# Third pair's loads behind the second pair's codes, and weight pieces 4 and 5 behind the first pair's, in a fused routing-attention and MLP kernel

## The chip, the cores and the metric

One core of a Trainium2 chip runs the whole kernel. The metric is device time in microseconds (us). The engines are called PE (TensorE, with PEld for its weight loads), DVE (VectorE), ACT (ScalarE), POOL (GpSimd) and SP (SyncE, which only issues DMAs here). Each runs its own instructions in the order in which the program lists them, and waits at an instruction until that one's inputs are there. So the program's order on each engine is part of the design, and this change moves that order about.

## The reference

Batch 4, 8 heads, 768 positions, head size 64, 16 clusters; d_model 512, d_ff 2048. Queries and keys are each assigned to the cluster whose centroid they resemble most, and a query attends only to keys of its own cluster. A two-layer block follows.

```python
q_assign = argmax(einsum('bhsd,hcd->bhsc', q_n, c_n))
k_assign = argmax(einsum('bhsd,hcd->bhsc', k_n, c_n))
mask = q_assign[:, :, :, None] == k_assign[:, :, None, :]
scores = where(mask, scale * (q @ k.T), -1e9)
attn = softmax(scores)
x = (attn @ v)            # heads side by side: (3072, 512)
h = x @ w_in
out = (h - tanh(h)) @ w_out
```

The weights come as 64-bit numbers, so a piece of them has to be turned into 32-bit numbers on the chip ("rounding").

## The kernel before

The work is tiled by pairs of heads: pair n is batch n // 4, heads 2p and 2p + 1. A pair's attention runs in six steps, written (n, half, s): half of the queries, and s = 0, 1, 2 for two 128-key blocks each. The list `steps` begins with the first halves of pairs 0 to 3 (steps 0 to 11), and one Python loop over it (L1031) writes out, for each step, the instructions of all engines in a fixed order. There is no scheduler: what the loop emits first on an engine runs first there.

A pair has to pass these stages before its steps:

- `load(n)` (L302): four DMAs on SP, 192 KB each, for q and k of both heads. In SBUF each head's rows are interleaved with the other's.
- `turn(n)` (L319): 12 PE transposes into two PSUM tiles `pt`, and two copies to SBUF (ACT for all but one).
- `similar(n)` (L337): PE products with the centroids, and an ACT copy.
- `route(n)` (L350): 3 PE transposes and four DVE operations, which leave each position's cluster code.
- `publish(n)` (L383): a PE transpose `pq`, a DVE cast, and a DMA on SP of the codes to DRAM (`q_codes`, 6 KB at most).
- `spread(0, 0)` (L398): for the first pair only, one DMA on SP brings the query codes back to all partitions as `row`. `select` (L467) then masks the exponentials on DVE.
- `spread_both(n)` (L406), for pairs 1 to 3: two DMAs on SP bring query and key codes back as `hot`; `one_hot(n)` (L414, DVE operations L418 and L422) turns them into factors, which PE adds to the scores (L454). A pair's scores cannot be finished before its `one_hot`.

A step of the loop emits, in this order: the scores of the next step (`begin`, L435, with ACT's exponentials L465), the ACT part of the day's weight pieces (`rest_of`), the products with v (`value`, `av`, L497), stage 0 (`turn`) if one is due, the sums of the weights (`sum_up`, `den`), then the rest: selects, the other stages, and the DVE part of the weight pieces (`round_piece`), each of which also fetches a piece three ahead through POOL's DMA queue (`fetch`, L209). `similar` (stage 1) comes ahead of the next step's scores.

When a stage is due stands in `ready` (L927 to L935): for pair n it is step `first_step + places[i]`, where i counts turn, similar, route, publish, spread_both, one_hot. Before the change the places of pair 2 are steps 0, 1, 1, 2, 2, 4, those of pair 3 steps 3, 4, 4, 5, 5, 7. The second pair's own stages are written out ahead of the loop, with `one_hot(1)` in step 1. For pair 3 `turn` also issues `load(4)` (L914). How many weight pieces are rounded in a step stands in `paces` (L1028).

The wait `gate` (L986) is a device that the kernel has already: a copy on POOL of one element of a loaded tile, so that the DMAs listed on POOL after it start only when that tile has landed. It holds the first three weight pieces behind the first pair's q and k.

Of the kernel before, what the change touches and what calls it, by code (L numbers as in the profile page):

```python
# [58 lines left out]
def kernel(  # L59
# [10 lines left out]
    nc = tc.nc  # L70
# [107 lines left out]
    def fast():  # L178
# [40 lines left out]
        def rest_of(at: int):  # L219
            if words == 2 and at < len(PIECES):  # L220
                rests[at] = restp.tile([P, FQ * P], U32, name="rest", tag="rest")
                added_words(PIECES[at][0], raws[at], rests[at])

        def round_piece(at: int):
            if words == 2:
                halved(PIECES[at][0], raws.pop(at), rests.pop(at))
            fetch(at + AHEAD)
# [74 lines left out]
        def load(n: int, what=(0, 1)):  # L302
            if n >= len(pairs):
                return
            b, p = pairs[n]
            for i in what:
                if i < 2:
                    pool, tag = (gp, "g") if b == 0 else (loads, f"x{i}")
                    t = raw_qk[n, i] = pool.tile([P, NCH, 2, D], F32, name=f"x{i}", tag=tag)
                else:  # L310
                    pool = vp0 if n in (2, 3) else vp
                    t = vals[n] = pool.tile([P, 2, NCH, D], F32, name="vals")
                for h in range(2):
                    nc.sync.dma_start(
                        t[:, :, h] if i < 2 else t[:, h],
                        (q, k, v)[i][b, 2 * p + h].rearrange("(p j) d -> p j d", p=P),
                    )
# [19 lines left out]
        def similar(n: int):  # L337

            ps = ps_f.tile([P, TB], F32, name="sim", tag="f")
            for i in range(2):  # L340
                for half in range(2):
                    r = (2 * i + half) * 2 * C
                    nc.tensor.matmul(  # L343
                        ps[r : r + 2 * C], lhsT=bd[:, pairs[n][1]],
                        rhs=turned[n, i][:, half], start=True, stop=True, tile_position=(0, r),
                    )
            sims[n] = rtp.tile([P, TB], F32, name="simt")
            nc.scalar.copy(out=sims[n], in_=ps)
# [25 lines left out]
        def summed(n: int, half: int):  # L374

            return n < HP and half == 0

        def masked(n: int, half: int):


            return summed(n, half) and n > 0

        def publish(n: int):  # L383

            sides = 2 if masked(n, 0) else 1
            G = HCH * 4 * sides
            ps = ps_f.tile([G, P], F32, name="pq", tag="f")
            nc.tensor.transpose(
                out=ps, in_=codes[n][:, 0:sides].rearrange("p i a h j -> p (i a h j)"), identity=ident
            )  # L390
            t = rtp.tile([G, P], BF16, name=f"qc{sides}")
            nc.vector.tensor_copy(out=t, in_=ps)
            q_codes[n] = dram.tile([sides, 2, 2, HCH * P], BF16, name=f"q_codes{sides}")
            nc.sync.dma_start(q_codes[n].rearrange("i a h (j p) -> (i a h j) p", p=P), t)

        rows, hots = {}, {}
# [9 lines left out]
        def spread_both(n: int):  # L406

            t = hots[n] = gp.tile([P, 2, 2, TB], BF16, name="hot", tag="g")
            for h in range(2):
                nc.sync.dma_start(  # L410
                    t[h * D : h * D + D], q_codes[n][:, :, h].unsqueeze(0).to_broadcast([D, 2, 2, TB])
                )
# [16 lines left out]
        def weight_tiles(n: int, half: int, s: int):  # L429
            if (n, half, s) == (0, 0, NS - 1):  # L430
                return [gp.tile([P, 2, TB], F32, name="e", tag="g") for _ in range(2)]
            t = ep.tile([P, 2, 2, TB], F32, name="e")
            return [t[:, i] for i in range(2)]

        def begin(step):  # L435
            n, half, s = step
            sc = {}
            for i in range(2):
                j = 2 * s + i
                sc[i] = ps_s.tile([P, 2, 512], F32, name="sc", tag="s")  # L440
                for h in range(2):
                    r = slice(h * D, h * D + D)
                    nc.tensor.matmul(  # L443
                        sc[i][:, h, 0:TB],
                        lhsT=turned[n, 1][r].rearrange("p a n -> p (a n)")[:, j * P : (j + 1) * P],
                        rhs=turned[n, 0][r, half], start=True, stop=not masked(n, half),
                    )
            for i in range(2):
                j = 2 * s + i
                out = sc[i][:, :, 0:TB]  # L450
                if masked(n, half):
                    for h in range(2):
                        r = slice(h * D, h * D + D)
                        nc.tensor.matmul(  # L454
                            sc[i][:, h, 0:TB],
                            lhsT=hots[n][r, 1].rearrange("p a n -> p (a n)")[:, j * P : (j + 1) * P],
                            rhs=hots[n][r, 0, half], start=False, stop=True,
                        )
                if summed(n, half):
                    if i == 0:  # L460
                        weights[n, half, s] = weight_tiles(n, half, s)
                    out = weights[n, half, s][i]
                else:
                    scores[n, half, j] = sc[i]
                nc.scalar.activation(out=out, in_=sc[i][:, :, 0:TB], func=ACT.Exp, scale=SCALE)  # L465
# [442 lines left out]
        def before(n: int):  # L908


            def turns():
                turn(n, 0, nc.scalar)
                turn(n, 1, nc.scalar)
                if n >= HP - 1:  # L914
                    load(n + 1)

            yield turns
            yield lambda: similar(n)
            yield lambda: route(n)
            yield lambda: publish(n)  # L920
            if masked(n, 0):
                yield lambda: spread_both(n)
                yield lambda: one_hot(n)
# [3 lines left out]
        ready = {}  # L927
        for n in range(2, len(pairs)):
            if n < HP:
                first_step, places = 3 * (n - 2), (0, 1, 1, 2, 2, 4)  # L930
            else:
                first_step = steps.index((n - 1, 0, 0) if n > HP else (n - 2, 1, 0))
                places = (-1, 0, 1, 3)
            for i, stage in enumerate(before(n)):
                ready.setdefault(first_step + places[i], {})[i] = stage  # L935
# [50 lines left out]
        gate = const.tile([P, 1], F32, name="gate")  # L986
# [13 lines left out]
        spread(0, 0)  # L1000
        rest_of(0)
        similar(1)
        load(2)
        rest_of(1)
        begin(steps[0])
        for _ in range(2):
            round_piece(rounding.pop(0))
        route(1)
# [1 line left out]
        begin(steps[2])  # L1010
        publish(1)
        spread_both(1)
        load(1, (2,))
        load(3)
        for n in range(2, HP):
# [9 lines left out]

        paces = dict(enumerate((0, 0, 1, 2, 0, 0, 2, 2, 1, 1, 1, 0, 3, 2, 2, 2, 2, 2, 2, 3, 2)))  # L1028
        late, divides, makers, later = [], [], [], {}
        fill, whole, spent, since, over = [], 0.0, 0.0, 0, 1  # L1030
        for at, (n, half, s) in enumerate(steps):  # L1031
# [108 lines left out]
        for t, bound in (  # L1140
# [7 lines left out]
            out=fits, in0=inverse, scalar1=MOST_INVERSE * words, scalar2=None, op0=ALU.is_le  # L1148
        )
        nc.vector.scalar_tensor_tensor(  # L1150
            out=fits, in0=inverse, scalar=words / SUM_MOST, in1=fits, op0=ALU.is_ge, op1=ALU.mult
        )
        checks = [fits, largest]
        if words == 2:
            nc.vector.tensor_scalar(
                out=smallest, in0=smallest, scalar1=HIGH_LEAST, scalar2=None, op0=ALU.is_ge
# [161 lines left out]
    with ExitStack() as cx, tc.manual_schedule():  # L1318
        fast()
# [35 lines left out]
```

## Time and profile before

| | us |
|---|---|
| three runs | 990.96, 991.83, 992.31 |
| median | 991.83 |
| span of the profiled execution | 990.3 |
| PE busy | 976.6 |
| PE weight loads | 467.0 |
| DVE busy | 531.4 |
| POOL busy | 499.7 |
| ACT busy | 321.7 |

A group's row in the profile gives start and length in us, engine, line, operation, output and inputs, how many instructions were merged, and in brackets how long the engine sat idle before and what ended that. SPq rows are DMA issues: their length is the time in which the queue took the descriptors, not that of the transfer. For these transfers the trace holds the moments at which each of a DMA's 16 shares reported completion; the last of them is its landing.

The 40 slices of the page are 24.8 us each. The change touches the first two or three.

### The profile page before, as it was taken

How to read it: one execution, taken by the hardware profiler on the slowest of the kernel's cores; microseconds unless marked ns; L12 is line 12 of the kernel's file. 1: busy time of each engine (PE TensorE's matmuls, PEld its weight loads, DVE VectorE, ACT ScalarE, POOL GpSimd, SP SyncE). 2: the span in 40 equal slices, each digit the busy share in tenths (PEclk: the TensorE clock that was granted, in tenths of full speed). 3: DMA queues.
4: the chain of work that ended last, by engine and by line, in shares of the span. 5: the costliest groups of instructions: out<-in, count | busy, mean ns of one | idle time of the engine just before them, and what ended most of it. 6: DMA issues, size and time to landing. Idle time of an engine off the chain costs nothing.

```text
span 990.3 us, 16579 instructions
## 1 busy us (share of the span) xinstructions
PE 976.6 (99%) x6444; PEld 467.0 (47%) x6444; DVE 531.4 (54%) x1017; ACT 321.7 (32%) x493; POOL 499.7 (50%) x346
## 2 busy tenths in 40 slices
PE   7999999999999999999999999999999999999997
PEld 4344443344443334444455555444455555444664
DVE  5547567448655667656554357655645336533011
ACT  5566564233442333343331222324341221122000
POOL 1015334444445464786777345676688345466600
PEclk9999999999999999999999999999999999999999
DMA  8854363125475724463536637344453232233321
GB/s 209 211 136 140 112 181 105 30 51 153 120 217 144 218 91 126 147 173 118 176 111 201 193 117 215 109 148 123 149 166 95 99 110 74 103 112 127 103 102 35
DMA packets 115977, 132.47 MB, mean 134 GB/s; under 512 B 62980, under 2 KB 95668, under 8 KB 113204
## 3 DMA queue, kind: packets, MB, share of 16 engines
q1 hardware_dynamic: 109508, 109.81, 37.3%
q0 software_dynamic: 6240, 21.50, 6.6%
q8 instruction: 53, 0.87, 0.4%
q14 instruction: 32, 0.26, 0.1%
q10 hardware_dynamic: 144, 0.03, 0.0%
HBM read 110.14 MB, written 21.17 MB: 133 GB/s over the span
## 4 chain that ended last, share of the span: by engine, by line
PE 96%; DVE 2%; DMA 1%; ACT 1%; issue 0%; POOL 0%; ACTq 0%; DVEq 0%
PE pd L855 22%; PE pu L804 21%; PE sc L443 14%; PE av L497 14%; PE o L628 8%; PE h L612 8%; PE pt L324 2%; PE den L537 2%; PE sim L343 1%; PE warm L294 1%; PE den L511 1%; DMA row<-q_codes 1%; PE pr L356 1%; DVE e L475 1%; PE den L518 0%
## 5 line engine op out<-in xcount | busy, mean ns | idle before, releaser
L488 POOL TENSOR_TENSOR sum<-sum,e 128x768 f32<-128x768 f32 x112 | 206.1, 1840 | 107.6 <-DVE e L475 103.8
L475 DVE SCALAR_TENSOR_TENSOR e<-row,code,sc 128x384 f32<-128x384 bf16 x336 | 185.2, 607 | 99.1 <-ACT sc L465 77.8
L855 PE MATMUL pd<-stream,G 128*64 128x256 f32 x1728 | 191.8, 379 | 0.0
L465 ACT ACTIVATE sc<-sc 128x768 f32<-128x768 f32 x168 | 125.9, 792 | 202.7 <-PE sc L443 187.9
L855 PEld LDWEIGHTS pd<-stream,G 128*64 128x64 f32 x1728 | 123.8, 137 | 67.4 <-issue 7.9
L443 PE MATMUL sc<-t,t 64*128 64x384 f32 x768 | 150.0, 509 | 0.9 <-ACT e L465 0.9
L497 PE MATMUL av<-e,vals 128*64 128x384 f32 x768 | 145.6, 498 | 1.8 <-DVE e L475 1.8
L799 POOL TENSOR_TENSOR G<-G,th 128x768 f32<-128x768 f32 (+1 forms) x51 | 88.0, 1738 | 98.6 <-ACT th L797 98.6
L804 PE MATMUL pu<-xT,stream 128*64 128x384 f32 x768 | 134.9, 488 | 0.7 <-DVE top L364 0.7
L804 PE MATMUL pu<-diff,stream 128*64 128x384 f32 x576 | 103.1, 487 | 0.0
L443 PEld LDWEIGHTS sc<-t,t 64*128 64x128 f32 x768 | 66.0, 186 | 74.8 <-issue 41.9
L484 POOL TENSOR_TENSOR sum<-e 128x768 f32<-128x768 f32 x28 | 56.8, 2028 | 74.6 <-DVE e L475 66.3
L804 PEld LDWEIGHTS pu<-xT,stream 128*64 128x64 f32 x768 | 54.1, 137 | 69.5 <-issue 62.5
L497 PEld LDWEIGHTS av<-e,vals 128*64 128x64 f32 x768 | 47.6, 136 | 83.1 <-issue 78.9
L612 PE MATMUL h<-xT,w_in 128*64 128x384 f32 x512 | 86.3, 487 | 0.1
L628 PE MATMUL o<-w_out,g 128*64 128x512 f32 x384 | 86.3, 594 | 0.0
L797 ACT ACTIVATE th<-G 128x768 f32<-128x768 f32 (+1 forms) x51 | 40.9, 806 | 117.6 <-DVE G L792 114.0
L804 PEld LDWEIGHTS pu<-diff,stream 128*64 128x64 f32 x576 | 40.8, 137 | 49.9 <-issue 44.5
L792 DVE TENSOR_TENSOR G<-pu,u 128x384 f32<-128x384 f32 x72 | 39.8, 552 | 41.4 <-PE pu L804 41.2
L612 PEld LDWEIGHTS h<-xT,w_in 128*64 128x64 f32 x512 | 36.4, 137 | 46.3 <-issue 44.7
L628 PEld LDWEIGHTS o<-w_out,g 128*64 128x64 f32 x384 | 27.1, 137 | 50.3 <-issue 49.6
L866 DVE SCALAR_TENSOR_TENSOR c<-pd,du 128x256 f32<-128x256 f32 x36 | 15.1, 420 | 62.5 <-PE pd L855 62.5
(123 smaller groups left out, 843.5 us busy)
## 6 DMA issues: line engine op xcount, KB each, us to landing
stream<-up_factors SPq DMA_DIRECT2D x24, 896.0 KB
stream<-down_factors SPq DMA_DIRECT2D x21, 1024.0 KB
raw<-in_moe_w_in_dram POOLq DMA_DIRECT2D x16, 512.0 KB, 5.8
raw<-in_moe_w_out_dram POOLq DMA_DIRECT2D x16, 512.0 KB, 5.2
again<-in_moe_w_in_dram SPq DMA_DIRECT2D x32, 256.0 KB
again<-in_moe_w_out_dram SPq DMA_DIRECT2D x32, 256.0 KB
x<-in_q_dram SPq DMA_DIRECT2D x32, 192.0 KB
x<-in_k_dram SPq DMA_DIRECT2D x32, 192.0 KB
```

The costliest lines, as they stand in the source:

```text
L443: nc.tensor.matmul(sc[i][:, h, 0:TB], lhsT=turned[n, 1][r].rearrange("p a n -> p (a n)")[:, j * P : (j + 1) * P], rhs=turned[n, 0][r, half ...
L465: nc.scalar.activation(out=out, in_=sc[i][:, :, 0:TB], func=ACT.Exp, scale=SCALE)
L475: nc.vector.scalar_tensor_tensor(out=e[:, h], in0=rows[n, half][:, h], scalar=codes[n][:, 1, j // HCH, h, j % HCH : j % HCH + 1], in1=sc[: ...
L484: nc.gpsimd.tensor_tensor(out=s, in0=pair[0], in1=pair[1], op=ALU.add)
L488: nc.gpsimd.tensor_tensor(out=s, in0=s, in1=pair[i], op=ALU.add)
L497: nc.tensor.matmul(avs[n, half][h * D : h * D + D], lhsT=vals[n][:, h, j], rhs=e[i][:, h], start=(j == 0), stop=(j == NCH - 1),)
L612: nc.tensor.matmul(h[r], lhsT=w_in[i][:, c, o * P : (o + 1) * P][:, r], rhs=xT[c][:, half], start=(c == 0), stop=(c == CD - 1),)
L628: nc.tensor.matmul(acc[sub][r], lhsT=gs[f % HF][:, f // HF, sub * P : (sub + 1) * P][:, r], rhs=w_out[f // FQ][:, f % FQ], start=(f == seq ...
L797: nc.scalar.activation(out=th, in_=t, func=ACT.Tanh)
L799: nc.gpsimd.tensor_tensor(out=t, in0=t, in1=th, op=ALU.subtract)
L804: nc.tensor.matmul(ps[r], lhsT=streams[base + i][:, c, k_, r], rhs=right[c], start=(c == 0), stop=(c == CH - 1),)
L855: nc.tensor.matmul(ps[r], lhsT=left(i)[:, r], rhs=t[:, i], start=(i == 0), stop=(i == HF - 1))
```

## The change

Four edits.

1. A second copy into `gate` on POOL reads the tile `row`. It stands ahead of the rounding of pieces 0 and 1, so the fetches that these trigger (the fourth and fifth weight piece) are issued after `row` has landed.
2. `load(2)` moves from behind `similar(1)` to behind `spread_both(1)`: on SP its four DMAs now follow the second pair's codes and both `hot` DMAs.
3. The stages of pair 2 start one step later: turn in step 1, similar and route in 2, publish and spread_both in 3; one_hot stays in step 4. Pair 3 keeps its steps. As a result publish(2) and its spread_both follow turn(3) and with it load(4).
4. The paces of steps 2, 3 and 4 become 2, 0, 1 instead of 1, 2, 0.

```diff
-                first_step, places = 3 * (n - 2), (0, 1, 1, 2, 2, 4)
+                first_step, places = 2 * n - 3, (0, 1, 1, 2, 2, 4 if n > 2 else 3)
...
         similar(1)
-        load(2)
         rest_of(1)
         begin(steps[0])
+
+        nc.gpsimd.tensor_copy(out=gate, in_=rows[0, 0][:, 0, 0:1])
         for _ in range(2):
             round_piece(rounding.pop(0))
...
         publish(1)
         spread_both(1)
+        load(2)
         load(1, (2,))
         load(3)
...
-        paces = dict(enumerate((0, 0, 1, 2, 0, 0, 2, 2, 1, 1, 1, 0, 3, 2, 2, 2, 2, 2, 2, 3, 2)))
+        paces = dict(enumerate((0, 0, 2, 0, 1, 0, 2, 2, 1, 1, 1, 0, 3, 2, 2, 2, 2, 2, 2, 3, 2)))
```

## The prediction

> **What bounds the kernel now.** I read the page's busy time and slices first, then a table of stretches of the first 60 us, then the timelines of TensorE, VectorE and the SyncE queue there. Page, parts 1 and 2:
>
> ```profile
> PE 976.6 (99%) x6444; PEld 467.0 (47%) x6444; DVE 531.4 (54%) x1017; ACT 321.7 (32%) x493; POOL 499.7 (50%) x346
> ...
> PE   7999999999999999999999999999999999999997
> ```
>
> TensorE (PE) is idle for 990.3 - 976.6 = 13.7 us, nearly all in the first and last slices. The stretches (length, then busy us of PE, PEld, DVE, ACT, POOL, then clock, DMA share, GB/s) place it:
>
> ```profile
> 21.00:24.00 3.00, 1.83 (x9) 0.69 (x9) 0.78 (x3) 2.20 (x3) 0.00 (x0) 1.00 1.05 290
> 24.00:27.00 3.00, 2.37 (x8) 0.77 (x8) 3.00 (x6) 0.00 (x0) 0.00 (x0) 1.00 1.00 233
> 27.00:30.00 3.00, 2.42 (x23) 1.60 (x24) 3.00 (x7) 1.41 (x2) 0.00 (x0) 1.00 0.05 10
> ...
> 42.00:45.00 3.00, 2.00 (x19) 0.81 (x17) 1.73 (x3) 3.00 (x5) 1.05 (x2) 1.00 0.95 235
> ...
> 48.00:60.00 12.00, 12.00 (x80) 4.85 (x80) 3.76 (x9) 7.17 (x12) 0.30 (x1) 1.00 0.46 113
> ```
>
> From 45 us to the tail PE never stops, so any microsecond that PE gains or loses before then moves the end by one. Four waits lie where the change works. The PE timeline:
>
> ```profile
> 24.63 2.45 PE L497 MATMUL av<-e,vals 128*64 128x384 f32 x8 [1.77 <-DVE e L475]
> 27.18 0.85 PE L324 MATMUL pt<-ident,x 128*128 128x128 f32 x6
> 28.50 0.85 PE L324 MATMUL pt<-ident,x 128*128 128x128 f32 x6 [0.47 <-issue]
> ...
> 44.54 1.54 PE L343 MATMUL sim<-t,bd 128*32 128x384 f32 x8 [1.00 <-ACT t L331]
> ```
>
> The first av waits for the selects, which wait for `row`. The two halves of turn(2) wait for load(2): the completion records of the trace put its last q quarter at 27.04 and its last k quarter at 28.41, where they start. sim(3) waits for ScalarE's copies of turn(3), behind two weight pieces. VectorE and the SP queue:
>
> ```profile
> 22.90 0.28 DVE L392 CAST qc<-pq 24x128 bf16<-24x128 f32 x1 [1.44 <-PE pq L388]
> 23.96 6.44 DVE L475 SCALAR_TENSOR_TENSOR e<-row,code,e 128x384 f32<-128x384 bf16 x12 [0.78 <-DMA row<-q_codes]
> ```
>
> ```profile
> 17.45 0.34 SPq L401 DMA_DIRECT2D row<-q_codes  x1
> 17.84 1.25 SPq L314 DMA_DIRECT2D x<-in_q_dram  x2
> 19.13 4.48 SPq L314 DMA_DIRECT2D x<-in_k_dram  x2
> 23.71 2.17 SPq L394 DMA_DIRECT2D q_codes<-qc  x1
> 29.21 1.28 SPq L410 DMA_DIRECT2D hot<-q_codes  x2
> ```
>
> The 6 KB q_codes(1) was issued at 23.71 and landed only at 29.2 (hot's issue waits for it), behind load(2); q_codes(0), alone in the queue, took 17.43 - 16.15 = 1.28. What stands ahead in the SP queue is the price of a code round trip here.
>
> [...] 5.5 us against 1.28 for q_codes, and `row` takes 6.42 with pieces 4 and 5 on the POOL queue, about 3.6 later with little beside it (112.0 to 115.7, completion records). [...] the q/k loads (256-byte packets) land one 192 KB quarter every 0.9 us, the first weight pieces 512 KB every 1.25 us.
>
> **The change part by part.** Compared at one point: the first hot weight load of step 6 (L454), at 51.60 before.
>
> *Gate on the row.* One POOL copy is added (0.18 us, the L987 row). Behind it on POOL stand only fetch(3) and fetch(4), the fourth and fifth piece. `row` then lands at 17.45 + 3.6 = 21.1, the pieces at about 26 and 27; ScalarE asks for them at step 2 or later, past 38, so this delay costs nothing. The gain is capped by VectorE's order: selects follow the cast that ends at 23.18. They start at 23.22, not 23.96: gain 0.74 (0 to 0.74). With the old lag of 0.67, av(0) starts at 23.9; selects of 6.44/12 = 0.54 pace it to 25.9; den(0) 0.78 and av(1) 1.44 follow at once: 28.1. Then PE comes to turn(2), now at step 1.
>
> *load(2) behind spread_both(1).* Its four DMAs pass q_codes(1) and both hot DMAs on SP. q_codes(1) goes at 23.2 and lands after 1.28 (idle) to 2.0 (as 38.38 to 40.4, beside other loads); I take 1.7 because the pieces run beside it: 24.9. Two hot issues take 1.28, so load(2) is issued from 26.2 to 28.9. hot lands after 3.7 and 4.6 (29.21 to 32.93 and 33.82 before): 28.6 and 29.5. The four quarters follow at 0.9: q complete at 31.3, k at 33.1. Best case, idle landing of q_codes and 3.4 for hot: 32.3; with pieces in the way 34.5. PE wanted q at 28.1, so this new wait is 3.2, and 1.0 more for k. It is in-order: den(1), sim(2), the scores of step 3 and everything later stand behind it. From 33.15: turn 0.7, den(1) 0.78, sim(2) until about 35.5 (after the copy of k), scores 1.49 and hot part 0.33: av(2) at 37.3. Before it was 35.60, with pr(2) (0.48) already done: loss 37.3 + 0.48 - 35.60 = 2.2. hot(1) itself comes early and is not waited for. The pool of the tiles is taken in another order too: the third pair's k tile is now the one that reuses the first pair's place, whose reader ended before 10; no cost.
>
> *Paces.* Steps 2, 3, 4 get 2, 0, 1 pieces, not 1, 2, 0. ScalarE after step 3's exponentials (38.7): two pieces 2 x 1.26, xT and den 0.87: 42.1; exponentials of step 4 to 43.5; no piece stands before the copies of turn(3), which end at 45.7. PE reaches sim(3) at 45.6 and waits 0.2. Before: 44.54. So 1.1 of the 2.2 comes back, and PE asks for hot(2) at 45.6 + (51.60 - 44.54) + 0.1 = 52.8: plus 1.2.
>
> *publish(2) one step later.* Now it comes after turn(3), and turn(3) issues load(4). On SP the order becomes: four list DMAs, load(4), q_codes(2), hot(2); before, q_codes(2) and hot(2) stood first. The list waits for den: 42.1, four issues 1.49: load(4) begins at 43.6. Pieces 6 and 7 are fetched beside it (their predecessors are rounded at about 43.5 and 44.7). Its last quarter landed 9.6 after its first issue before (43.32 to 52.94, with hot(2) ahead and two pieces beside it); load(3), without pieces, took 6.8. Service alone is 4 x 0.9 + 2 x 1.25 = 6.1, and about 2 until data flow: I take 8.2, so 51.8. q_codes(2) lands 0.74 later (28.41 to 29.15 before): 52.5. hot(2) needs 4.24 (56.51 to 60.75 before): 56.8. The one-hot operations take 0.65 and hand over in 0.1: 57.6. PE wanted it at 52.8 and now waits 4.8; queued behind on VectorE stands route(3), 2.3 us, done before PE asks for its codes after av(5) and den(5).
>
> Sum at the mark: 57.6 - 51.60 = +6.0. Against the profile's own span this is 990.3 to 996.3; the unprofiled times are 990.96 to 992.31, median 991.83, so 997.8. Ends: 6.8 for load(4) and 0.8 less before it give +3.8; 9.6 and 1.4 more give +8.8. This case's own range is 995.6 to 1000.6. No later wait is there to absorb it.
>
> **The rivals.** *R1, only turn(2) waits:* if q_codes(2) passes load(4) rather than queueing behind it, or load(4) drains at once, hot(2) is there by 52.8 and the sum is +1.2: 993.0. For it: q_codes(1) and (2) are tiny. Against: the 5.5 us at 23.71. It decides when load(4) lands within about 3.5 us of its first issue; none did in under 6.8.
>
> *R2, faster:* load(2) arrives as PE comes to turn(2). Then the gains are 0.74 (selects), 0.55 and 0.47 (both turn waits), 1.0 (sim(3)), if hot(2) is in time too: 2.8 off, 989.0. For it: these waits are real and PE pays for each. Against: k would have to land at 28.8, as its last quarter is being issued; no q or k load has landed in under 3.4 us.
>
> **How the numbers follow.** My case, both waits: 0.78, 997.8. R1: 0.11, 993.0, mostly within 0.2% (989.8 to 993.8), which is about what a measurement of this kernel can tell from no change. R2: 0.10, 989.0. Something worse: 0.01. Range 993.0 to 1000.5: it leaves out R2, half of R1 and the top of my case. Faster 0.10, same 0.07, slower 0.83 (0.78 + 0.01 and the upper part of R1).
>
> **What would show it.** Right: selects at 23.2; turn(2)'s transposes starting near 31.4 and 33.1 instead of 27.2 and 28.5; no wait on ScalarE's copy before sim(3); VectorE idle before the second L418 until about 57 with the DMA hot as releaser, and PE idle some 5 us before L454. Wrong: turn(2) before 30, or the second L418 before 53; then the SP queue drains faster than its quarters of 0.9 us say, and the sum falls to R1 or R2.

## The result, and the profile after

| | us |
|---|---|
| before, median of 5 | 991.83 (990.96 to 992.31) |
| changed, median of 5 | 1002.91 (1002.48 to 1003.79) |
| ratio | 1.0113, 95% interval 1.0099 to 1.0128 |
| span of the profiled execution | 1001.1, before 990.3 |

The change costs 11 us, 1.1%. The direction was forecast, the size (997.8, at most 1000.5) was not. The page after, parts 1 and 2:

```profile
PE 979.3 (98%) x6444; PEld 468.2 (47%) x6444; DVE 529.2 (53%) x1017; ACT 321.6 (32%) x493; POOL 501.6 (50%) x347
...
PE   8779999999999999999999999999999999999997
```

PE's idle time grows from 13.7 to 1001.1 - 979.3 = 21.8 us, and the growth lies in the second and third slices. PE's busy time grows too, by 2.7 us, with the same 6444 matmuls. The table of stretches says why. Its columns: length, busy us of PE, PEld, DVE, ACT, POOL, granted PE clock, DMA share, GB/s.

```profile
28.30:33.50 5.20, 0.08 (x2) 0.00 (x0) 1.82 (x5) 0.00 (x0) 0.00 (x0) 0.75 1.13 206
33.50:38.60 5.10, 4.81 (x28) 2.91 (x28) 0.00 (x0) 1.60 (x2) 0.00 (x0) 0.59 1.26 251
...
55.70:61.00 5.30, 0.01 (x2) 0.06 (x1) 0.53 (x2) 0.00 (x0) 0.00 (x0) 0.74 0.34 75
61.00:65.00 4.00, 3.83 (x16) 1.14 (x20) 3.51 (x9) 1.71 (x3) 0.49 (x1) 0.50 0.02 1
```

There are two stretches in which PE stands still, and behind each some 4 us of work at half clock. The PE timeline names the waits:

```profile
23.71 2.45 PE L497 MATMUL av<-e,vals 128*64 128x384 f32 x8 [0.90 <-DVE e L475]
...
26.87 1.51 PE L497 MATMUL av<-e,vals 128*64 128x384 f32 x8
33.61 1.51 PE L324 MATMUL pt<-ident,x 128*128 128x128 f32 x6 [5.23 <-DMA x<-in_q_dram]
35.30 1.51 PE L324 MATMUL pt<-ident,x 128*128 128x128 f32 x6 [0.18 <-DMA x<-in_k_dram]
...
48.85 0.85 PE L343 MATMUL sim<-t,bd 128*32 128x384 f32 x8
...
61.17 0.82 PE L454 MATMUL sc<-hot 64*128 64x384 bf16 x4 [5.46 <-DVE hot L422]
61.93 2.83 PE L497 MATMUL av<-e,vals 128*64 128x384 f32 x8
```

Before, step 6 began like this:

```profile
51.92 0.49 PE L454 MATMUL sc<-hot 64*128 64x384 bf16 x4
52.34 1.51 PE L497 MATMUL av<-e,vals 128*64 128x384 f32 x8
```

The first av is 0.9 us earlier than before and sim(3) waits for nothing, as meant. But the transposes of turn(2) start at 33.6 and 35.3 (27.2 and 28.5 before), and the first hot product of step 6 at 61.17 (51.92 before). The transposes take 1.51 us, not 0.85, and the av at 61.93 takes 2.83, not 1.51, because both run at half clock (0.50 granted from 33.50 to 36.80 and from 61.00 to 65.00). VectorE and the SP queue:

```profile
22.85 0.28 DVE L392 CAST qc<-pq 24x128 bf16<-24x128 f32 x1 [1.44 <-PE pq L388]
23.06 6.42 DVE L475 SCALAR_TENSOR_TENSOR e<-row,code,e 128x384 f32<-128x384 bf16 x12
...
60.47 0.42 DVE L418 TENSOR_SCALAR hot<-hot,mine_code 128x768 bf16<-128x768 bf16 x1 [11.23 <-DMA hot<-q_codes]
```

```profile
23.15 0.31 SPq L394 DMA_DIRECT2D q_codes<-qc  x1
27.03 1.28 SPq L410 DMA_DIRECT2D hot<-q_codes  x2
28.36 1.30 SPq L314 DMA_DIRECT2D x<-in_q_dram  x2
...
45.23 1.12 SPq L550 DMA_DIRECT2D list<-den  x4
46.39 1.24 SPq L314 DMA_DIRECT2D x<-in_q_dram  x2
47.67 2.74 SPq L314 DMA_DIRECT2D x<-in_k_dram  x2
50.51 1.93 SPq L394 DMA_DIRECT2D q_codes<-qc  x1
55.98 1.27 SPq L410 DMA_DIRECT2D hot<-q_codes  x2
```

The selects now follow the cast at once. The chain that ended last (start, length, what) runs through the DMAs that the change moved:

```profile
23.15 3.86 DMA q_codes<-qc
...
30.61 4.56 DMA x<-in_k_dram
...
50.51 5.42 DMA q_codes<-qc
...
56.64 3.80 DMA hot<-q_codes
```

### The profile page after: what moved, and what is told of

Read it like the earlier page. It is cut to its first block, busy times and chain, and to the rows that moved or that the text cites. A ratio compares the mean times of both kernels' runs of the same rounds, so it can differ in the third digit from the quotient of the medians.

```text
span 1001.1 us, 16583 instructions
## 1 busy us (share of the span) xinstructions
PE 979.3 (98%) x6444; PEld 468.2 (47%) x6444; DVE 529.2 (53%) x1017; ACT 321.6 (32%) x493; POOL 501.6 (50%) x347
## 4 chain that ended last, share of the span: by engine, by line
PE 94%; DMA 2%; DVE 2%; SPq 1%; ACT 1%; issue 0%; POOL 0%; ACTq 0%
PE pd L855 22%; PE pu L804 21%; PE sc L443 14%; PE av L497 13%; PE o L628 8%; PE h L612 8%; PE pt L324 2%; PE den L537 2%; PE sim L343 1%; DMA q_codes<-qc 1%; PE warm L294 1%; PE den L511 1%; SPq L314 1%; PE pr L356 1%; DMA x<-in_k_dram 0%; DVE e L475 0%
```

## The experiments

My theory was this: PE waits twice, for load(2) behind the codes and for the codes behind load(4), and each wait of 5 us is followed by work at half clock. The rivals stand in the expectations. Each kernel was timed beside the kernel before on its own chip, so ratios are compared, and waits are read from traces.

### One edit alone: the gate

```diff
         begin(steps[0])
+        nc.gpsimd.tensor_copy(out=gate, in_=rows[0, 0][:, 0, 0:1])
```

> The kernel before with the first edit alone (the gate copy on POOL ahead of pieces 4 and 5). Theory: the row lands near 21 instead of 23.9 and load(2), no longer beside two weight pieces, lands by about 26, so the selects start at 23.2 (0.7 us gained) and both halves of turn(2) lose their waits (0.5 + 0.5 us): about 990.1 us, 1 to 2 us below before. Rival: the pieces only move their transfer on to q_codes(1) and hot(1), which then come late for step 3, and nothing is gained: 991.8 or more.

990.09 us, ratio 0.9987 (0.9979 to 0.9995). A small gain, as the theory had it: PE's first wait for the selects falls to 0.90 us, and both waits before turn(2) are gone. The price named by the rival is there, but it falls where there was slack: q_codes(1), behind load(2) in its queue and beside the two pieces, took from 22.78 to 27.34, the last of the two pieces landed at 27.00 (completion records), and yet PE waits for no hot product.

### One edit alone: the paces

```diff
-(0, 0, 1, 2, 0, 0, 2, 2, ...
+(0, 0, 2, 0, 1, 0, 2, 2, ...
```

> The kernel before with the fourth edit alone (paces 2, 0, 1 in steps 2 to 4). Theory: sim(3) no longer waits 1.0 us for the copies of turn(3) behind two pieces on ScalarE: about 990.8 us, 0.8 to 1.2 below before. Rival: with two pieces in step 2 ScalarE delays the exponentials of step 4 by 1.3 us and turn(3) with them, so the wait only moves: 991.8.

991.05 us, ratio 0.9995 (0.9988 to 1.0002): no difference shown. Both texts are wrong on how. sim(3) does lose its wait (0.2 left), and turn(3) is not late. In the traced execution the gain is given back 20 us later, as its PE timeline shows:

```profile
65.35 0.50 PE L454 MATMUL sc<-hot 64*128 64x384 bf16 x4 [1.26 <-DVE hot L422]
...
71.26 1.51 PE L497 MATMUL av<-e,vals 128*64 128x384 f32 x8 [0.87 <-ACT xT L528]
```

A piece that moved to step 4 is rounded there at 54 and so fetches another at 54.64, and two more go at 58.35 and 59.66, all beside hot(3), which lands at about 64.6. Before, no piece was fetched between 44.2 and 59.7, and hot(3) landed at 60.75. Where pieces are rounded also sets where they are fetched. The traced execution took 993.12 us, the second longest of 21, so it shows where the gain can go, and not how much of it goes in most executions.

### One edit alone: pair 2's stages a step later

```diff
-                first_step, places = 3 * (n - 2), (0, 1, 1, 2, 2, 4)
+                first_step, places = 2 * n - 3, (0, 1, 1, 2, 2, 4 if n > 2 else 3)
```

> The kernel before with the third edit alone (pair 2's stages one step later; load(2), paces and pieces where they were). Theory: turn(2) at step 1 finds load(2) landed, so its two waits of 0.5 us go, but publish(2) now stands behind load(4) on SP and hot(2) comes 4 to 5 us late, with 1.5 us at half clock behind it: 995 to 997. Rival (the lateness of hot(2) comes only with the other edits): 992 or less.

993.73 us, ratio 1.0027 (1.0015 to 1.0040): slower, but by about half of what I expected. The mechanism is there, smaller: PE waits 1.67 us for hot(2), and the clock doesn't fall (1.00 from 46 to 58 us; PE waits 0.64 us for hot(1) too).

```profile
53.30 0.50 PE L454 MATMUL sc<-hot 64*128 64x384 bf16 x4 [1.67 <-DVE hot L422]
```

With the old paces only one piece is fetched beside load(4), 1.3 us after it began. The expectation had taken over a size that belonged to the new paces; the run with the old paces, further down, tests that in the changed kernel.

### Put back: load(2)

```diff
         similar(1)
+        load(2)
         rest_of(1)
...
         spread_both(1)
-        load(2)
         load(1, (2,))
```

> The changed kernel with load(2) put back behind similar(1), all else as changed. Theory (order in the SP queue, plus the halved clock after a long wait): the wait before turn(2) goes (5.2 + 0.2 us) and with it about 1.8 us of transposes and sums at half clock; the wait for hot(2) stays: 995 to 996.5 us. Rival (the shifted stages of pair 2 and the paces cost by themselves, through ScalarE and VectorE): 1001 us or more.

995.47 us, ratio 1.0037 (1.0024 to 1.0051). The wait before turn(2) is gone and the one for hot(2) stays, as the theory said:

```profile
53.10 0.50 PE L454 MATMUL sc<-hot 64*128 64x384 bf16 x4 [4.94 <-DVE hot L422]
```

So the move of load(2), with the other three edits in place, costs some 7 us of the 11.

### Put back: hot(2) ahead of load(4)

```diff
                 turn(n, 1, nc.scalar)
-                if n >= HP - 1:
+                if n >= HP:
                     load(n + 1)
...
-                yield lambda: spread_both(n)
+                def codes_back():
+                    spread_both(n)
+                    if n == HP - 2:
+                        load(HP)
+                yield codes_back
```

> The changed kernel with load(4) issued after the third pair's codes and hot DMAs instead of inside turn(3), all else as changed. Theory (order in the SP queue): q_codes(2) lands about 1.5 us after its cast instead of 7, hot(2) is there when PE asks for it, and the wait of 5.5 us goes with about 1.9 us at half clock: 995 to 996.5 us. Rival (hot(2) is late because publish(2) itself comes a step later): the wait shrinks by less than 2 us: 1001 us or more.

1001.29 us, ratio 1.0093 (1.0078 to 1.0108). Neither was right: the wait for hot(2) falls from 5.5 to 2.8, yet only 1.6 us are won. The clock still falls (0.50 from 58 to 60 us), and a new wait of 1.7 us (av, for the copy of xT on ACT) comes later.

```profile
57.98 0.82 PE L454 MATMUL sc<-hot 64*128 64x384 bf16 x4 [2.80 <-DVE hot L422]
58.73 2.63 PE L497 MATMUL av<-e,vals 128*64 128x384 f32 x8
```

And q_codes(2), with no load of q or k ahead of it in its queue, still took 3.5 us (48.73 to 52.27).

### Put back: both, and then without pieces beside the codes

The first kernel has both edits above. The second also has

```diff
-(0, 0, 2, 0, 1, 0, 2, 2, ...
+(0, 0, 0, 0, 0, 1, 3, 3, ...
```

> The changed kernel with both SP orders mended: load(2) back behind similar(1), and load(4) behind the third pair's codes and hot DMAs. Theory (two separate waits that add up): what the second mending was worth with the first wait still there, 1.6 us, comes off the 995.5 of the first alone: about 993.9; PE still waits some 2.8 us for hot(2), because q_codes(2) and hot(2) go beside two weight pieces and start a step later. Rival (the waits hide one another): below 992, no wait for hot(2).

> As the kernel with both orders mended, but no weight piece is rounded in steps 2 to 4 (paces 0, 0, 0, 1, 3, 3 in steps 2 to 7), so that none is fetched beside q_codes(2) and hot(2). Theory (the fetched pieces share the DMA engines with the codes' round trip): q_codes(2) lands in under 2 us instead of 3.5, hot(2) is in time, and the wait of 2.8 us with its slow clock is gone: about 4 us below the kernel with both orders, unless the pieces that now crowd steps 5 to 7 make hot(3) late, which the trace would show. Rival (one step later is too late by itself): the wait for hot(2) stays above 2 us.

Both orders: 993.19 us, ratio 1.0017 (1.0010 to 1.0024), 2.9 us of wait for hot(2), as expected within 1 us. Without the pieces beside the codes: 996.27 us, ratio 1.0059 (1.0043 to 1.0074). The SP queue of the first, then of the second:

```profile
41.30 0.29 SPq L394 DMA_DIRECT2D q_codes<-qc  x1
44.83 1.27 SPq L410 DMA_DIRECT2D hot<-q_codes  x2
```

```profile
41.45 0.29 SPq L394 DMA_DIRECT2D q_codes<-qc  x1
42.79 1.27 SPq L410 DMA_DIRECT2D hot<-q_codes  x2
```

The same 6 KB, at the same place of the same queue, take 3.5 us beside two weight pieces and 1.3 without, and the wait for hot(2) falls from 2.9 to 0.2. So one step later is not too late by itself. The time did not fall by the 4 us that I expected, it rose by 3: three pieces in each of steps 6 and 7 hold up ACT's exponentials, and PE waits 4.4 us for them. That kernel answers its question by its trace, not by its time.

### Fill the waits

```diff
+            if (n, i) == (2, 0):
+                keep_warm(9)
             pt = ps_s.tile([P, 2, 512], F32, name="pt", tag="s")
...
                 if masked(n, half):
+                    if (n, half, s, i) == (2, 0, 0, 0):
+                        keep_warm(9)
                     for h in range(2):
```

> The changed kernel with nine idle matmuls (the kernel's own keep_warm) written into each of the two long waits of PE, ahead of turn(2) and ahead of the first hot product of step 6; they compute nothing that is used. Theory (a wait of 5 us halves PE's clock, and the work after it pays 1.7 to 1.9 us each time): the clock stays at 1.0 and the time falls to about 999.3. Rival (the halved clock costs nothing of note, the waits alone make up the 11 us, or the filling overruns the waits): 1002.5 or more.

999.82 us, ratio 1.0086 (1.0072 to 1.0099), about 3 us below the changed kernel. Its stretches, to be read beside those above:

```profile
33.50:38.60 5.10, 4.31 (x34) 2.39 (x36) 0.00 (x0) 2.08 (x3) 0.00 (x0) 1.00 1.24 252
...
61.00:65.00 4.00, 4.00 (x31) 1.62 (x29) 2.39 (x8) 2.23 (x5) 0.93 (x1) 1.00 0.15 37
```

The clock stays at 1.00. PE does more work and the kernel ends earlier, so the halved clock was worth about 3 of the 11 us.

### The changed kernel without the gate

The first edit undone.

> The changed kernel with its first edit undone: no second gate, so pieces 4 and 5 are fetched from 17 on again; the rest as changed. Theory ([...] the gate moves the pieces from the row onto q_codes(1)): q_codes(1) lands 1.3 to 2 us after its issue instead of 3.9, load(2) and with it turn(2) come about 2 us earlier, the wait before turn(2) is near 3 us instead of 5.2, and the time falls to 999 to 1000.5. The row lands by 23.5 and costs little. Rival (the gate is what frees the row, and without it the selects start at 24 or later as before, which delays everything): 1002.5 or more.

1001.95 us, ratio 1.0101 (1.0084 to 1.0118), whose interval overlaps that of the changed kernel, so no gain in time is shown. In the trace:

```profile
22.05 0.31 SPq L394 DMA_DIRECT2D q_codes<-qc  x1
24.48 1.29 SPq L410 DMA_DIRECT2D hot<-q_codes  x2
```

q_codes(1) takes 2.4 us instead of 3.9 and the wait before turn(2) is 3.8 instead of 5.2. But the second half of turn(2) now waits 0.85 us for ACT's copy of the first, the clock falls all the same (0.50 from 32 to 36 us), and PE stays at half of it until well into step 3's scores (the 8 products take 2.34 us, against 1.56). From the first av to the first hot product of step 3 PE takes 16.5 us, against 16.3 in the changed kernel, so what q_codes(1) won was lost again by then. The selects still follow the cast with no wait: once load(2) is out of the way, the row needs no gate.

### The changed kernel with the old paces

The fourth edit undone.

> The changed kernel with its fourth edit undone (paces 1, 2, 0 in steps 2 to 4). Theory (the new paces start two weight pieces together with load(4), ahead of q_codes(2) in time, and these hold both back): only one piece runs beside load(4), hot(2) comes 2 to 3 us earlier, the wait of 5.5 us shrinks to about 2.5 and with it the slow clock behind it; sim(3) waits 0.8 us again: 998.5 to 1000.5. Rival (the wait for hot(2) is due to load(4) ahead in the queue and to the later publish alone, and the paces give the 1 us at sim(3)): 1003 to 1004.

999.86 us, ratio 1.0091 (1.0063 to 1.0119); the interval is too wide to show the gain, but the trace has what was expected:

```profile
60.03 0.50 PE L454 MATMUL sc<-hot 64*128 64x384 bf16 x4 [2.31 <-DVE hot L422]
```

The wait is 2.3 us instead of 5.5, with full clock behind it (the av that follows takes 1.51 us, not 2.83), and sim(3) waits 0.8 again. But only a part of the 3.2 us is due to the fetches, as the theory had it. Counted from the first hot product of step 3, PE asks for hot(2) 1.5 us later than in the changed kernel, because sim(3) waits for the copies again, and the hot product itself comes only 1.6 us earlier. ACT hands over the list (`den`) 1.2 us earlier, with one piece less to round ahead of it, and hot(2) is issued 2.2 us earlier (54.23, against 55.98). That leaves some 1.0 us for the pieces beside the DMAs.

### A version that beats both

The kernel before, with the gate, and with the ACT part of the pieces written behind the copies of turn; the paces stay.

```diff
-            for piece in todays[:2]:
-                rest_of(piece)
             if not values_first:
                 value(n, half, s)
-            if summed(n, half):
-                if 0 in stages:
-                    stages.pop(0)()
+            if summed(n, half) and 0 in stages:
+                stages.pop(0)()
+            for piece in todays[:2]:
+                rest_of(piece)
+            if summed(n, half):
```

> The kernel before with the first edit alone, and the ACT part of a step's weight pieces written behind the copies of turn instead of ahead of them; the paces are those of before. Theory: sim(3) loses its wait of 1.0 us as with the changed paces, but the pieces are fetched within 1.5 us of where they were, so hot(3) is not made late: about 989.0, 1 us below the gate alone. Rival (what is won at sim(3) is given back at hot(3) or at the copies of xT as with the changed paces): 990 or more.

988.32 us, ratio 0.9968 (0.9960 to 0.9976): below both kernels. sim(3) starts without its wait of 1.0 us:

```profile
40.42 0.85 PE L518 MATMUL den<-e,ones 128*32 128x384 f32 x8
41.09 1.18 PE L343 MATMUL sim<-t,bd 128*32 128x384 f32 x8
```

and since the pieces are fetched nearly where they were, hot(3) is not waited for and the copy of xT costs 0.4 us. One wait of 0.3 us for hot(1) is left in step 3. This kernel has two of the change's aims without its moves on the SP queue.

## Why the prediction was wrong in size

The mechanism stands as far as it went: the likeliest case, both waits, came in the places and from the queue order that were named. What failed are two terms of the sum, the landing of q_codes(1) beside the gated pieces, put at 1.7 us, and the half-speed work behind the waits, put at nothing. The sum at the mark was +6.0 and came out at 61.17 - 51.92 = +9.25; a further 1.5 us comes behind the mark. By its steps:

- *Selects.* Forecast at 23.22, came at 23.06; av(1) ended at 28.3, forecast 28.1. Right.
- *The gate costs nothing.* This step failed. The delay of the two pieces cost ACT nothing, as said, but they then ran beside q_codes(1). I gave q_codes(1) 1.7 us to land, 0.4 of it for the pieces; it took 3.87. Everything behind it (hot(1), load(2)) was 2.2 us late: turn(2)'s second half came at 35.3, not 33.1. The transfer rate after that was right (0.9 us a quarter: the first three landed at 32.57, 33.48 and 34.38). What this step cost in time is counted, not shown: the kernel without the gate lost the gain again on the way to step 3.
- *Why a tiny DMA is so slow there.* With two pieces in flight q_codes was done 0.2 to 0.8 us after the second piece (27.03 after 26.27; with the gate alone 27.34 after 27.00; with both orders mended 44.83 after 44.61), and 1.3 us after its issue with none. The packets of the trace show where most of that time goes. The DMA view of the changed kernel, for 23.20 to 25.10 us and then for 25.10 to 26.00, has these queues (q0 carries POOL's transfers, q1 those of SP; packets, MB, share):

```profile
q0 software_dynamic: 186, 0.70, 96.5%
...
q0 software_dynamic: 49, 0.14, 37.4%
q1 hardware_dynamic: 36, 0.01, 3.8%
```

Until 25.10 no packet of q_codes(1) has moved, 2 us after its issue. Its data packets run from 25.14 to 25.93, nearly each pair of them directly (within 0.03 us) behind a packet of a piece. With no piece in flight (the second kernel with both orders) the last of them ended 0.9 us after the issue, as did those of q_codes(0) in the kernel before (17.08, issued at 16.15); here it was 2.8. So of the 2.5 us that the landing took longer, 1.9 are the codes' own packets standing behind the pieces, and at most 0.7 lies between the last packet and the report of completion; what makes up that rest, no run separates.

- *The work behind the wait.* This term was missing altogether. I priced turn(2), den(1), sim(2) and the scores at full clock. The mean granted clock was 0.59 and 0.50 in the stretches behind both waits. It fell 2.5 us into each wait (30.90 and 58.20) and came back 4.1 and 3.9 us after work had begun again (37.72 and 65.03). Filling the waits gave back 3 us. I had two waits of 4 to 5 us in my own sum and did not ask what they do to the clock.
- *Paces.* The wait at sim(3) goes, as said (48.85, no wait). That a moved piece moves a fetch, I used for load(4) but not beyond.
- *publish(2) behind load(4).* Forecast wait 4.8, measured 5.5. q_codes(2) landed at 55.95: 3.5 us after the forecast, most of it inherited, since the list that opens the chain left ScalarE at 45.2 and not 42.1. load(4) to q_codes(2): 46.39 to 55.95 is 9.6, where 8.2 + 0.74 was taken. The order in the queue is about half of this wait (2.8 us are left without it). With the old paces 2.3 us are left, but there only some 1.0 us is due to the pieces beside the DMAs.

In sum, at the mark: 6.0 forecast, 2.2 for q_codes(1), and 1.0 for half-speed work behind turn(2) (5.1 us from its second half to the av of step 3, where 4.15 was taken) make 9.2, against 9.25. Behind the mark another 1.5 us at half speed follow, and the spans differ by 10.8. R1 fell because q_codes(2) did come behind load(4) (the last k quarter landed at 55.76, the codes 0.2 us later); and even with load(4) moved behind it, PE still waited 2.8 us. R2 fell because even the first half of load(2) landed 5 us after PE was ready for it.

## What to carry to other kernels

Before a load is moved behind a small round trip on the same queue, count when its last byte lands against when the in-order engine will ask. Here the move freed the row, which the gate alone does too (0.9 us at the first av in either case), and it cost a wait of 5.2 us. A gate that frees one transfer puts the gated ones beside the next; ask which small DMA is issued while they run (here q_codes(1), 3.9 us in the changed kernel and 2.4 without its gate). And price a wait of PE with the half-speed work that may follow it: in the changed kernel the clock fell 2.5 us into both waits, and filling them won 3 us.

## What the runs showed that was not expected

- A DMA of 6 KB took 1.3 us from issue to landing with no weight piece under way, and 3.5 to 3.9 us when two 512 KB pieces were under way on another queue and no load stood ahead of it on its own.
- The clock does not fall at one fixed length of wait: one of 2.80 us (hot(2) ahead of load(4)) was followed by products at half speed, one of 2.85 us (both orders mended) by products at full speed:

```profile
50.60 0.50 PE L454 MATMUL sc<-hot 64*128 64x384 bf16 x4 [2.85 <-DVE hot L422]
51.03 1.51 PE L497 MATMUL av<-e,vals 128*64 128x384 f32 x8
```

The granted clock was 0.50 from 58 to 60 us behind the first, and 1.00 from 47 to 53 us, through the second and behind it. With load(2) put back the clock held at 1.00 from 48 to 53 us, through the wait of 4.94 us, and was 0.62 and 0.53 in the two stretches of 2 us behind it. What decides when it falls, these runs do not show.

- The wait for hot(2) is 1.7 us with the shifted stages alone, and 4.9 with gate, stages and paces (no run has the stages and the paces without the gate). As with the old paces above, 1.5 us of the difference is PE asking earlier, since sim(3) no longer waits, and most of the rest is the list leaving ACT later; the fetches are the smaller part.
